# Attention and feed-forward on one core: softmax denominators of several tiles in one step, a joint transpose of the tails, another planned order

## The chip, the cores and the metric

The kernel runs on one core of one Trainium2 chip. The metric is the device time of one execution in microseconds (us), the median of three runs. Before the change it is 660.17 us (659.78 to 661.85).

## What is computed

First attention for 4 batches of 8 heads, 576 positions of 64 features, causal, mixed with a linear memory term by a gate of each head. Then a feed-forward network from 512 over 2048 back to 512 features, with a rational activation, on all 2304 tokens.

```python
def _attn_ref(q, k, v, M_prev, z_prev, beta):
    scores = scale * np.matmul(q, k.transpose(0, 1, 3, 2))
    scores = np.where(causal, -1000000000.0, scores)
    scores = scores - scores.max(-1, keepdims=True)
    a = np.exp(scores)
    a /= a.sum(-1, keepdims=True) + 1e-09
    local = np.matmul(a, v)
    q_p = phi(q)                       # x + 1 above zero, exp(x) below
    mem_out = einsum(q_p, M_prev) / (einsum(q_p, z_prev) + 1e-06)
    return g * mem_out + (1 - g) * local

def _moe_ref(x, w_in, w_out, a, b):
    h = x @ w_in
    P = a[0] + a[1] * h + a[2] * h * h + a[3] * h * h * h
    Q = 1.0 + np.abs(b[0]) * np.abs(h) + np.abs(b[1]) * h * h
    return (P / (Q + 1e-06)) @ w_out
```

The weights of the feed-forward network come as 64-bit floats.

## The kernel before

Attention works on 16 **units**, a unit being two heads of one batch. `load` fetches a unit. `prep` turns q and k with matmuls against the identity (tile `idf`) into `kt`, and makes the memory term's `f` out of `E` (exp), `nk` (reused for relu) and `den` (the normaliser). The 576 queries of a head are four tiles of 128, t = 0 to 3, and a tail of 64. `tiles01` does t = 0 and 1, `tile23` does 2 and 3 one by one, and `tail` does the 64 last queries of both heads together.

`prob` is the softmax of one tile of one head. A DVE instruction (`TENSOR_TENSOR_REDUCE`, shown as `ISA` or `CUSTOM_DVE_ANT_0`) masks and takes the extreme, and a second one reads the accumulator into the small tile `st`. ACT takes the exponential (`P` or the smaller `Ps`) with its sum. POOL or DVE adds 1e-9 and multiplies with the head's gate (L617, L618). DVE takes the reciprocal (L620). POOL, ACT or DVE multiplies the row with it (L621 to L623). PE turns the result (L476), a copy brings it to `g`, and `av` multiplies with v and the memory term and leaves the unit's outcome in `x`, which `spill` stores to DRAM (`xs`).

The feed-forward network works in two **halves** of eight of the 16 slices of 2048. For every slice `weights` makes two 32-bit parts of a weight (`ta`, `tw`, `xf`, a PSUM bank). `group` loads 256 tokens (`xload`), multiplies (`ffn1`), runs the activation (`act_chain`, 36 chains in the first half and 36 in the second), multiplies with the second weight (`ffn2`), and stores a partial sum `po`. The second half adds to it and writes the result. With `full` set, `act_chain` computes one factor with an ACT instruction (L828) and a POOL product (L492), else with one DVE instruction (L498). `FULL = 4` sets it for all groups from the fourth in the first half; the second half always has it.

The order is not written by hand. `Sched.place` is a planner. It knows a price for every operation (`c_act`, `c_dve`, `c_pool`, `c_mm4` ...) and a priority (`PRI`), puts the operation first that can start first, chooses among the engines that an operation may run on by its price times one plus `BIAS`, and so lays down one instruction queue for each engine. Each queue is then run in that order. SP issues all DMAs, in its own queue.

## Time and profile before

| | us |
|---|---|
| median of 3 runs | 660.17 |
| the profiled execution | 659.89 |
| its span, first to last instruction | 658.1 |

| engine | busy us | share of the span |
|---|---|---|
| PE (matmul) | 630.4 | 96% |
| DVE | 530.2 | 81% |
| ACT | 444.0 | 67% |
| POOL | 452.1 | 69% |

The span has three parts. Until about 160 us there is attention alone, with the splitting of the first half's weights beside it. Until about 290 us attention and the first matmuls of the feed-forward network are mixed. From then on there is the network alone, to 658 us. A busy PE is not a PE at its peak: matmuls overlap, and a slow stream of them can count as busy. How many start in a stretch says more.

### The profile page before, as it was taken

How to read it: one execution, taken by the hardware profiler on the slowest of the kernel's cores; microseconds unless marked ns; L12 is line 12 of the kernel's file. 1: busy time of each engine (PE TensorE's matmuls, PEld its weight loads, DVE VectorE, ACT ScalarE, POOL GpSimd, SP SyncE). 2: the span in 40 equal slices, each digit the busy share in tenths (PEclk: the TensorE clock that was granted, in tenths of full speed). 3: DMA queues.
4: the chain of work that ended last, by engine and by line, in shares of the span. 5: the costliest groups of instructions: out<-in, count | busy, mean ns of one | idle time of the engine just before them, and what ended most of it. 6: DMA issues, size and time to landing. Idle time of an engine off the chain costs nothing.

```text
span 658.1 us, 11480 instructions
## 1 busy us (share of the span) xinstructions
PE 630.4 (96%) x3744; PEld 496.7 (75%) x3744; DVE 530.2 (81%) x1229; ACT 444.0 (67%) x987; POOL 452.1 (69%) x553
## 2 busy tenths in 40 slices
PE   5999989789999999999999999999999999999997
PEld 3656555446776777788999999998998888888876
DVE  4899999986997775958999979789887767677765
ACT  3899799787789787664575766677465555372671
POOL 3778688886665755744677979888766666475563
PEclk9999999799999999999999999999999999999999
DMA  5644755557231421226464334222771110300301
GB/s 116 167 125 118 197 161 155 170 140 205 75 90 35 126 79 37 85 80 234 151 193 142 117 126 160 81 81 96 282 297 31 64 65 1 127 2 0 129 0 65
DMA packets 89276, 75.74 MB, mean 115 GB/s; under 512 B 62592, under 2 KB 75392, under 8 KB 86912
## 3 DMA queue, kind: packets, MB, share of 16 engines
q1 hardware_dynamic: 89216, 75.00, 36.9%
q8 instruction: 30, 0.49, 0.3%
q14 instruction: 30, 0.25, 0.1%
HBM read 51.39 MB, written 23.59 MB: 114 GB/s over the span
## 4 chain that ended last, share of the span: by engine, by line
PE 74%; DVE 9%; ACT 7%; POOL 5%; issue 2%; DMA 2%; SPq 1%; POOLq 0%; ACTq 0%; DVEq 0%
PE bk L465 68%; PE bk L476 6%; DVE bk L605 2%; ACT Ps L609 1%; ACT g L470 1%; ACT P L609 1%; POOL Ps L621 1%; DMA xf<-in_moe_w_in_dram 1%; SPq L458 1%; POOL nk L492 1%; DVE E L498 1%; POOL st L617 1%; DVE tb L819 1%; POOL E L492 1%; DVE bk L783 1%
## 5 line engine op out<-in xcount | busy, mean ns | idle before, releaser
L465 PE MATMUL bk<-xg,w 128*128 128x256 f32 x864 | 111.0, 285 | 0.0
L465 PEld LDWEIGHTS bk<-xg,w 128*128 128x128 f32 x864 | 106.8, 191 | 2.7 <-issue 1.5
L492 POOL TENSOR_TENSOR tw<-tw,gh 128x512 f32<-128x512 f32 x56 | 72.8, 1301 | 42.2 <-DVE gh L498 37.8
L814 POOL TENSOR_SCALAR tw<-ta,cb 128x512 f32<-128x512 f32 x68 | 53.7, 789 | 63.7 <-ACT ta L810 63.6
L492 POOL TENSOR_TENSOR tw<-tw,ta 128x512 f32<-128x512 f32 x72 | 94.0, 1306 | 4.3
L465 PE MATMUL bk<-w,gh 128*128 128x512 f32 x288 | 90.5, 395 | 0.0
L810 ACT ACTIVATE ta<-bk 128x512 f32<-128x512 f32 x72 | 43.0, 597 | 68.8 <-PE bk L465 32.8
L465 PE MATMUL bk<-w2o,gh 128*128 128x512 f32 x288 | 88.7, 390 | 0.0
L605 DVE CUSTOM_DVE_ANT_0 bk<-bk,mk 128x384 f32<-128x384 f32 (+3 forms) x144 | 71.5, 520 | 8.2 <-PE bk L465 8.0
L818 ACT ACTIVATE ta<-tw,lnb 128x512 f32<-128x512 f32 x72 | 52.0, 722 | 33.9 <-POOL tw L492 33.5
L819 DVE TENSOR_TENSOR tb<-bk,tb 128x512 f32<-128x512 f32 x72 | 49.3, 686 | 30.6 <-ACT tb L811 25.9
L498 DVE SCALAR_TENSOR_TENSOR bk<-bk,ca,tw 128x512 f32<-128x512 f32 x72 | 54.2, 753 | 18.7 <-POOL tw L492 18.4
L465 PE MATMUL bk<-w,w2i 128*128 128x512 f32 x288 | 67.7, 390 | 0.0
L470 ACT COPY g<-bk 128x384 f32<-128x384 f32 (+2 forms) x128 | 58.2, 496 | 7.4 <-PE bk L476 6.4
L821 DVE SCALAR_TENSOR_TENSOR bk<-tb,ca,bk 128x512 f32<-128x512 f32 x72 | 54.0, 750 | 11.3 <-ACT ta L810 10.5
L465 PEld LDWEIGHTS bk<-w,w2i 128*128 128x128 f32 x288 | 53.9, 188 | 11.7 <-DVE gl L834 0.5
L811 ACT ACTIVATE tb<-bk,ca 128x512 f32<-128x512 f32 x59 | 45.6, 773 | 24.1 <-PE bk L465 23.9
L465 PEld LDWEIGHTS bk<-w2o,gh 128*128 128x128 f32 x288 | 53.6, 188 | 10.7
L465 PEld LDWEIGHTS bk<-w,gh 128*128 128x128 f32 x288 | 52.2, 188 | 11.4 <-issue 1.1
L498 DVE SCALAR_TENSOR_TENSOR gh<-bk,ca,ta 128x512 fp32r<-128x512 f32 x72 | 53.5, 743 | 8.5 <-ACT ta L823 4.5
L465 PE MATMUL bk<-w2o,gl 128*128 128x512 f32 x144 | 56.1, 390 | 1.2 <-DVE gl L834 1.2
L465 PE MATMUL bk<-w,gl 128*128 128x512 f32 x144 | 56.1, 389 | 0.0
(123 smaller groups left out, 1413.4 us busy)
## 6 DMA issues: line engine op xcount, KB each, us to landing
xh<-xg SPq DMA_DIRECT2D x9, 1024.0 KB, 5.0
xf<-in_moe_w_in_dram SPq DMA_DIRECT2D x16, 512.0 KB, 4.3
xf<-in_moe_w_out_dram SPq DMA_DIRECT2D x16, 512.0 KB, 3.4
w<-xh SPq DMA_DIRECT2D x6, 1024.0 KB, 11.9
xs<-x SPq DMA_DIRECT2D x16, 288.0 KB, 2.2
xf<-xs SPq DMA_DIRECT2D x9, 512.0 KB, 6.1
po<-tb SPq DMA_DIRECT2D x18, 256.0 KB, 2.8
pi<-po SPq DMA_DIRECT2D x18, 256.0 KB, 2.8
```

The lines of the kernel that those rows point to most:

```text
L465: T.matmul(o, lhsT=l, rhs=r, start=s0, stop=s1, skip_group_check=more)
L470: sc.op([("act", c_act(n), lambda: A.copy(out=out(), in_=in_())), ("dve", c_dve(n), lambda: V.tensor_copy(out(), in_()))], reads, writes, pri)
L476: T.matmul(o, lhsT=i, rhs=idn, start=x == 0, stop=True, is_transpose=True, skip_group_check=x > 0)
L492: opts = {"pool": ("pool", c_pool2(n), lambda: G.tensor_tensor(**kw()), "t"), "dve": ("dve", c_dve(n), lambda: V.tensor_tensor(**kw()), "2")}
L498: return dve(c_dve(n) + 61 * ap, lambda: V.scalar_tensor_tensor(out=out(), in0=in0(), scalar=scalar() if callable(scalar) else scalar, in1 ...
L605: V.tensor_tensor_reduce(out=s, in0=s, in1=m, scale=-0.125, scalar=st.t[:, 0:1] if x else 3.0e38, op0=ALU.add, op1=ALU.min, accum_out=st.t ...
L810: act(c_act(N), lambda: A.activation(a_(), h(), AF.Abs), [(hb, None)], [(ta, None)], p)
L811: sc.op([("act", c_act(N, ap=2), lambda: A.activation(b_(), h(), AF.Identity, scale=ca[:, 3:4], bias=ca[:, 2:3])), ("dve", c_dve(N) + 61, ...
L814: sc.op([("pool", c_pool(N, 2), lambda: G.tensor_scalar(w_(), a_(), cb[:, 1:2], cb[:, 0:1], op0=ALU.mult, op1=ALU.add), "s"), ("act", c_ac ...
L818: act(c_act(N, False, 1), lambda: A.activation(a_(), w_(), AF.Ln, scale=2.0 ** -63, bias=lnb[:, 0:1]), [(tw, None)], [(ta, None)], p)
L819: dve(c_dve(N), lambda: V.tensor_tensor(out=b_(), in0=h(), in1=b_(), op=ALU.mult), [(hb, None)], [(tb, None)], p)
L821: dve(c_dve(N) + 61, lambda: V.scalar_tensor_tensor(out=h(), in0=b_(), scalar=ca[:, 1:2], in1=h(), op0=ALU.add, op1=ALU.mult), [(tb, None) ...
```

## The change

`prob` now takes a list of tiles. For t = 0 and 1 the four tiles of both heads share one `st`, and one DVE instruction (L630, `SCALAR_TENSOR_TENSOR`) adds 1e-9 to all four sums and multiplies with the gates, and one reciprocal (L632) serves all four. For t = 2 and 3 two tiles share them. This step is now on DVE alone. The tails of q and k are loaded into one tile `kq` (k in the upper half, q in the lower half) and turned with one matmul in the place of two. q's tail is loaded once more into `nq`, for the exponential. `x` becomes `x0` and `x1`, each stored as soon as it is there. One weight operation (an absolute value) may run on DVE too. `FULL` is 10, so that the first half's chains all take the DVE instruction. The planner's price of a pair of matmuls of two heads loses a surcharge of half (`1.5 * c_mm4(n)` becomes `c_mm4(n)`), and `BIAS` and `PRI` are new numbers, in a loop over half units.

```diff
-BIAS = {'act': 1.73, 'dve': 2.43, 'pool': -0.41}
+BIAS = {'act': 0.23, 'dve': 2.22, 'pool': -2.16}
...
+        for i, src in enumerate((k, q)):
+            dma(lambda i=i, src=src: (kq.t[64 * i:64 * i + 64].rearrange("p (a d) -> p a d", a=2), src[bb, h2, SM:S, :].rearrange("a p d -> p a d")),
+                [], [(kq, i)], pri, 64 * 512, 256)
...
-        tr(lambda: [(b4(tl)[:, x, :], ad(s, 4), idf) for x, s in enumerate((nk, nq))],
-           2 * 109, [(nq, None), (nk, None)], [(tl, None)], p, [kt, qd])
+        tr(lambda: [(tl.t[:, 0:128], kq.t, idf)], 109, [(kq, None)], [(tl, None)], p, [kt, qd])
...
-        sc.op([("pool", c_pool(1, 1), lambda: G.tensor_scalar(st.t[:, 4:5], st.t[:, l], 1e-9, gcol, op0=ALU.add, op1=ALU.mult), "s"),
-               ("dve", 130, lambda: V.tensor_scalar(st.t[:, 4:5], st.t[:, l], 1e-9, gcol, op0=ALU.add, op1=ALU.mult))],
-              [(st, ("l", mx))], [(st, "r")], p)
-        dve(75, lambda: V.reciprocal(st.t[:, 5:6], st.t[:, 4:5]), [(st, "r")], [(st, "i")], p)
...
+        def den():
+            x = col(1).rearrange("p (t i) -> p t i", i=gcol.shape[1])
+            y = col(2).rearrange("p (t i) -> p t i", i=gcol.shape[1])
+            V.scalar_tensor_tensor(out=y, in0=x, scalar=1e-9, in1=gcol.unsqueeze(1).to_broadcast(list(x.shape)), op0=ALU.add, op1=ALU.mult)
+        dve(130, den, [(st, ("l", 0, k)) for k in range(w)], [(st, "r")], p)
+        dve(75, lambda: V.reciprocal(col(3), col(2)), [(st, "r")], [(st, "i")], p)
...
-        mm(f, 1.5 * c_mm4(n) + 100, [(kt, "k"), (kt, "q")], [(x, None) for x in bk], p, take=P[0] + P[1])
...
+            mm(f, c_mm4(n) + 100, [(kt, "k"), (kt, "q")], [(x, None) for x in bk], p + t, take=P + [st])
...
-        x = d["x"] = d.get("x") or sc.buf("x")
-        copy(n, lambda: x.t[:, q0:q0 + n], lambda: o.t[:, 0:n], [(o, None)], [(x, ch)], p)
...
+        x = sc.buf(f"x{ch}")
+        copy(n, lambda: x.t, lambda: o.t[:, 0:n], [(o, None)], [(x, None)], p)
+        dma(lambda: (xs[c, :, bb * S + q0:bb * S + q0 + n], x.t), [(x, None)], [(ex(("xs", bb, ch)), c)], p, 128 * n * 4)
...
-FULL = 4
+FULL = 10
...
-PRI = {'load': 21.6, 'head': 19.6, 'av0': 13.5, 'prep': 46.6, 't2': 52.0, 'tail': 15, 'av1': 75.9, 'w': 50.2, 'w2': 3401.0, 'group': 218.5, 'chain': 10.9, 'ahead': 366.1, 'ahead2': 6071.5, 'last': 3553.7}
+PRI = {'load': 4.5, 'head': 2.3, 'av0': 13.2, 'prep': 25.3, 't2': 14.8, 't3': 2.5, 'tail': -9.4, 'av1': 42.9, 'w': 100.2, 'w2': 6715.7, 'group': 227.8, 'chain': 22.8, 'ahead': 329.1, 'ahead2': 2903.3, 'last': 1385.4}
```

Three places of the order show what moves. The first is DVE's queue in the softmax of a middle unit; `st` is the tile of sums, `g` the gates. Before:

```order
L618 TENSOR_SCALAR st_166<-st_166,g_92 128x1
L605 ISA bk_113,st_170<-bk_113,mk 128x512
L605 ISA st_170 128x1
L620 RECIPROCAL st_166<-st_166 128x1
L620 RECIPROCAL st_167<-st_167 128x1
L605 ISA bk_118,st_170<-bk_118,mt,st_170 128x64
L605 ISA st_170 128x1
L781 TENSOR_SCALAR bk_115<-ta_179 128x512
L620 RECIPROCAL st_168<-st_168 128x1
```

After:

```order
L807 TENSOR_SCALAR bk_115<-ta_179 128x512
L809 SCALAR_TENSOR_TENSOR bk_115<-xf_194,bk_115 128x512
L630 SCALAR_TENSOR_TENSOR st_162<-st_162,g_92 128x4
L614 ISA bk_116,st_166<-bk_116,mk 128x512
L614 ISA st_166 128x1
L632 RECIPROCAL st_162<-st_162 128x4
L614 ISA bk_113,st_166<-bk_113,mk 128x512
L614 ISA st_166 128x1
```

Four gate steps (this one on DVE, the others on POOL) and four reciprocals became one of each, four columns wide. In the whole program the reciprocals fall from 144 to 64, the gate steps from 144 (62 on DVE, 82 on POOL) to 64, all on DVE.

The second place is POOL's queue, where a unit's rows are multiplied with the reciprocal. Before:

```order
L621 TENSOR_SCALAR P_149<-P_149,st_162 128x512
L621 TENSOR_SCALAR P_150<-P_150,st_163 128x512
L617 TENSOR_SCALAR st_164<-st_164,g_92 128x1
L621 TENSOR_SCALAR Ps_153<-Ps_153,st_159 128x128
L617 TENSOR_SCALAR st_165<-st_165,g_92 128x1
L621 TENSOR_SCALAR Ps_155<-Ps_155,st_164 128x128
L621 TENSOR_SCALAR Ps_154<-Ps_154,st_165 128x256
L617 TENSOR_SCALAR st_166<-st_166,g_92 128x1
```

After:

```order
L506 TENSOR_SCALAR w_177<-tw_186 128x512
L494 TENSOR_TENSOR w_177<-tw_186,w_177 128x512
L636 TENSOR_SCALAR Ps_157<-Ps_157,st_163 128x128
L636 TENSOR_SCALAR Ps_158<-Ps_158,st_163 128x128
L636 TENSOR_SCALAR Ps_155<-Ps_155,st_163 128x256
L636 TENSOR_SCALAR P_153<-P_153,st_167 128x512
L636 TENSOR_SCALAR P_152<-P_152,st_167 128x512
```

The small gate steps are gone from POOL's queue, and the products of a group of tiles stand in a row.

The third place is PE's queue at the end of attention (`mz`, `nv`: the last products of the last unit; `xg,w`: first matmuls of the feed-forward network; `w,gh`: its second ones). Before:

```order
L465 MATMUL bk_113<-xg_195,w_177 128x256 x12
L465 MATMUL bk_114<-xg_195,w_177 128x256 x24
L476 MATMUL bk_115<-idf,P_152 128x128 x4
L476 MATMUL bk_116<-idf,P_150 128x128 x4
L465 MATMUL bk_112<-xg_195,w_177 128x256 x12
L465 MATMUL bk_111<-f_144,mz_138 128x320
L465 MATMUL bk_111<-g_174,vt_130 128x64
L465 MATMUL bk_111<-g_174,nv_128 64x320 x6
L465 MATMUL bk_111<-g_174,nv_128 64x192 x2
```

After:

```order
L467 MATMUL bk_113<-w_177,gh_187 128x512 x2
L467 MATMUL bk_113<-w_177,gl_190 128x512
L467 MATMUL bk_117<-f_146,mz_140 128x320
L467 MATMUL bk_117<-g_172,vt_132 128x64
L467 MATMUL bk_117<-g_172,nv_130 64x320 x6
L467 MATMUL bk_117<-g_172,nv_130 64x192 x2
L467 MATMUL bk_118<-xg_195,w_177 128x256 x24
L467 MATMUL bk_114<-xg_195,w_177 128x256 x24
L467 MATMUL bk_111<-xg_195,w_177 128x256 x24
```

Before its last attention matmul PE had 252 feed-forward matmuls of 256 columns and 48 of 512 columns in its queue; now it has 96 and 9. The others moved behind attention.

## Rows read from the trace of the kernel before

**Rows 1.** Stretches of the span, all engines; columns named in the first row.
```profile
core 0: us, PE busy (x) PEld busy (x) DVE busy (x) ACT busy (x) POOL busy (x), PEclk, DMA share, GB/s
...
20.00:80.00 60.00, 58.15 (x379) 36.69 (x379) 54.58 (x189) 52.13 (x156) 45.30 (x73) 1.00 0.57 148
80.00:140.00 60.00, 51.09 (x299) 30.58 (x299) 57.33 (x183) 51.74 (x151) 50.53 (x74) 0.94 0.60 169
140.00:160.00 20.00, 18.03 (x118) 11.17 (x117) 14.96 (x63) 15.72 (x53) 17.31 (x27) 1.00 0.59 164
160.00:290.00 130.00, 128.34 (x870) 93.75 (x871) 101.06 (x322) 101.10 (x271) 79.43 (x123) 1.00 0.28 80
290.00:480.00 190.00, 190.00 (x1216) 172.47 (x1215) 164.74 (x246) 119.99 (x191) 146.01 (x137) 1.00 0.44 152
480.00:614.00 134.00, 134.00 (x649) 113.17 (x648) 96.10 (x140) 70.22 (x108) 78.32 (x71) 1.00 0.21 75
```

**Rows 2.** The chain that ended last: start us, us, what.
```profile
207.52 2.80 PE bk L476 x24
...
289.59 325.15 PE bk L465 x1868
...
627.27 27.22 PE bk L465 x118
```

**Rows 3.** Waits of DVE, 80 to 140 us: us in total, times, longest.
```profile
DVE st L620 <- POOL st L617: 0.7, 3, 0.4
```

**Rows 4.** DVE groups by line and form: count, busy us, mean ns, idle before.
```profile
L620 DVE RECIPROCAL st<-st 128x1 f32<-128x1 f32 x144 | 20.9, 154 | 8.1 <-POOL st L617 7.2
...
L498 DVE SCALAR_TENSOR_TENSOR tw<-tw,gh 128x512 f32<-128x512 f32 x16 | 15.2, 949 | 0.3
...
L618 DVE TENSOR_SCALAR st<-st,g 128x1 f32<-128x1 f32 x58 | 11.3, 202 | 3.2 <-ACT Ps L609 2.7
...
L812 DVE TENSOR_SCALAR tb<-bk,ca 128x512 f32<-128x512 f32 x13 | 10.5, 807 | 8.1 <-ACT ta L810 7.7 <-PE bk L465 0.2
...
L575 DVE TENSOR_SCALAR nk<-nq 128x640 f32<-128x640 f32 x12 | 6.9, 577 | 0.4 <-PE bk L476 0.2
L623 DVE TENSOR_SCALAR Ps<-Ps,st 128x128 f32<-128x128 f32 x8 | 5.0, 626 | 0.0
L615 DVE TENSOR_TENSOR st<-st 128x1 f32<-128x1 f32 x16 | 4.9, 305 | 1.7 <-ACT P L609 1.7
L623 DVE TENSOR_SCALAR Ps<-Ps,st 128x256 f32<-128x256 f32 x6 | 4.8, 796 | 0.0
```

**Rows 5.** Line L615: instructions' duration in ns, min/median/max.
```profile
L615 DVE TENSOR_TENSOR st<-st x16: 135/156/1301, 16.6 to 247.3; 128x1 f32<-128x1 f32 x16
```

**Rows 6.** ACT and POOL groups, same columns as rows 4.
```profile
L811 ACT ACTIVATE tb<-bk,ca 128x512 f32<-128x512 f32 x59 | 45.6, 773 | 24.1 <-PE bk L465 23.9
L828 ACT ACTIVATE tw<-tw,lnb 128x512 f32<-128x512 f32 x56 | 39.7, 710 | 0.0
...
L574 ACT ACTIVATE nk<-nq 128x640 f32<-128x640 f32 x4 | 3.1, 766 | 0.0
...
L492 POOL TENSOR_TENSOR tw<-tw,gh 128x512 f32<-128x512 f32 x56 | 72.8, 1301 | 42.2 <-DVE gh L498 37.8 <-ACT ta L810 2.8 <-ACT ta L818 1.6
...
L617 POOL TENSOR_SCALAR st<-st,g 128x1 f32<-128x1 f32 x70 | 20.2, 288 | 28.0 <-ACT Ps L609 9.6 <-ACT P L609 9.1 <-DMA nv<-in_v_dram 4.5
```

**Rows 7.** SP's queue near the start: start us, us of issuing, what.
```profile
2.55 1.91 SPq L458 DMA_DIRECT2D nk<-in_k_dram  x3
```

**Rows 8.** PE's timeline at 401 us: 24 matmuls of 256 columns, until the next.
```profile
400.97 3.04 PE L465 MATMUL bk<-xg,w 128*128 128x256 f32 x24
403.84 0.63 PE L465 MATMUL bk<-w,gh 128*128 128x512 f32 x2
```

**Rows 9.** All engines, 520 to 540 us, 512-column matmuls alone; columns as rows 1.
```profile
520.00:540.00 20.00, 20.00 (x90) 16.57 (x89) 12.52 (x19) 10.43 (x16) 10.97 (x11) 1.00 0.12 40
```

More of the change, by code (lines that the diff above doesn't have):

```diff
@@ L563, in prep @@
             r = slice(64 * i, 64 * i + 64)
[L564 removed]
+            copy(64, lambda r=r: qd.t[r, r], lambda r=r: tl.t[r, 64:128], [(tl, None)], [(qd, i)], p)
         for src, n, c0 in ((nk, "k", 0), (nq, "q", S)):
@@ L640, in tiles01 @@
     def tiles01(u, p):
         d = ST[u]
-        P = [scores(u, t, p + t) for t in range(2)]
+        P = scores(u, (0, 1), p)
         g = d["g0"] = sc.buf("g0")
@@ L654, in tile23 @@
         n = 128 * (t + 1)
-        P = scores(u, t, p)
+        P = scores(u, (t,), p - t)
         if "g1" not in d:
@@ L704, in f @@
             return [(a_, l, r, x == 0, x == len(L) - 1) for x, (a_, l, r) in enumerate(L)]
-        mm(f, c_mm4(n) + sum(c_mm4(n - o0) for o0 in blk) + 0.5 * c_mm4(n) + (c_mm4(64) if ch else 0) + 100,
+        mm(f, c_mm4(n) + sum(c_mm4(n - o0) for o0 in blk) + (c_mm4(64) if ch else 0) + 100,
            [(g, None), (nv, None), (vt, None), (mz, None), (F, None)], [(o, None)], p, more=True)
-        x = d["x"] = d.get("x") or sc.buf("x")
-        copy(n, lambda: x.t[:, q0:q0 + n], lambda: o.t[:, 0:n], [(o, None)], [(x, ch)], p)
@@ L710, in spill @@
-    def spill(u, p):
-        bb, c = divmod(u, KC)
-        x = ST[u]["x"]
-        dma(lambda: (xs[c, :, bb * S:(bb + 1) * S], x.t), [(x, None)], [(ex(("xs", bb)), c)], p, 128 * S * 4)
-    pr = PRI
-    load(0, -1)
-    prep(0, 0)
-    for u in range(U):
-        base = 100.0 * u
-        if u + 1 < U:
-            load(u + 1, base + pr["load"])
-        tiles01(u, base + 10)
-        av(u, 0, base + pr["av0"])
-        if u + 1 < U:
-            prep(u + 1, base + pr["prep"])
-        for t in range(2, 4):
-            tile23(u, t, base + pr["t2"] + pr["head"] * (t - 2))
-        tail(u, base + pr["tail"])
-        av(u, 1, base + pr["av1"])
-        spill(u, base + pr["av1"] + 2)
+        x = sc.buf(f"x{ch}")
@@ new lines, in av @@
+        copy(n, lambda: x.t, lambda: o.t[:, 0:n], [(o, None)], [(x, None)], p)
+        dma(lambda: (xs[c, :, bb * S + q0:bb * S + q0 + n], x.t), [(x, None)], [(ex(("xs", bb, ch)), c)], p, 128 * n * 4)
+    pr = PRI
+    units = []
+    for bb in range(NB):
+        us = range(KC * bb, KC * bb + KC)
+        units += [(x, u) for x in "AB" for u in us] if bb < SWEEPS else [(x, u) for u in us for x in "AB"]
+    pos = [j for j, x in enumerate(units) if x[0] == "A"]
+    load(0, -100)
+    prep(0, -60)
@@ new lines, in tile_attention_ffn @@
+    for at, (kind, u) in enumerate(units):
+        base = 50.0 * at
+        for j in pos:
+            if j and at == j - (1 if j - 1 in pos else 2):
+                load(units[j][1], base + pr["load"])
+            if j and j - 1 == at and kind == "B":
+                prep(units[j][1], base + pr["prep"])
+        if kind == "A":
+            tiles01(u, base + pr["head"])
+            av(u, 0, base + pr["av0"])
+            if at + 1 in pos:
+                prep(units[at + 1][1], base + pr["prep"])
+        else:
+            for t in range(2, 4):
+                tile23(u, t, base + pr["t2"] + pr["t3"] * (t - 2))
+            tail(u, base + pr["tail"])
+            av(u, 1, base + pr["av1"])
@@ L839, in xload @@
         xf, xg = sc.buf(tf), sc.buf(tg)
-        rd = [(ex(("xs", bb)), None) for bb in range(t0 // S, (t0 + 255) // S + 1)]
+        rd = {(x // S, int(x % S >= 256)) for x in (t0, t0 + 255)}
+        rd |= {(b1, c1) for b1, _ in rd for c1 in range(2) if t0 < b1 * S + 256 * (1 + c1) + 64 * c1 and t0 + 256 > b1 * S + 256 * c1}
+        rd = [(ex(("xs", *x)), None) for x in sorted(rd)]
         dma(lambda: (xf.t, xs[:, :, t0:t0 + 256].rearrange("c p s -> p c s")), rd, [(xf, None)], p, 128 * KC * 1024)
```

109 lines of the change are left out of this document (61 added, 48 removed).

## The prediction

> **What bounds the kernel now.** I read the stretches first, for every engine side by side. From 290 to 614 us PE is busy all the time [rows 1], and the chain of waits there is one piece of 325 us of matmuls [rows 2]. So the last part is bound by PE, and nothing that another engine gains in it is worth anything. What can be won lies before 290 us.
>
> There PE's busy share misleads: 58.2 of 60 us, 51.1 of 60, 128.3 of 130 [rows 1]. Busy counts slow streams too, so I count matmul starts. Both stretches from 20 to 80 and from 80 to 140 us hold attention alone, in about the same mixture. The first starts 379 matmuls (6.3 in a us), the second 299 (5.0 in a us) [rows 1]. At the first pace 299 matmuls take 47.3 us, so 12.7 of the 60 us are lost against it; the 118 of 140 to 160 us lose another 1.3. Who is late? From 80 to 140 us DVE is busy 57.3 of 60 us, ACT 51.7, POOL 50.5 [rows 1], and DVE hardly waits: the longest row of its waits there is 0.7 us [rows 3]. DVE sets the pace of this middle, where the splitting of the weights stands beside the softmax. From 20 to 80 us it is closer: DVE 54.6, ACT 52.1 [rows 1], and neither has much to spare. From 160 to 290 us PE is busy all but 1.7 us, with feed-forward matmuls as filling.
>
> **The change part by part.** My base is the profiled execution, 659.9 us (a span of 658.1 and 1.8 around it); the median of the runs is 0.3 above it.
>
> *PE.* One transpose less in each of 16 units: 24 transposes in a row take 2.80 us [rows 2], 0.117 each, so 16 take 1.9 us. PE waits for none of it elsewhere, so I take it in full: **-1.9**. Everything else on PE is the same work in another order.
>
> *The moved feed-forward matmuls.* Before the last attention matmul PE had 252 of 256 columns and 48 of 512; now 96 and 9. 24 of the first kind take 2.87 us until the next instruction starts [rows 8], 0.120 each; 90 of the second take 20 us [rows 9], 0.222 each. 156 x 0.120 + 39 x 0.222 = 27.4 us that leave the stretch before 290 us and come back behind it, where PE never waits. The sum is nothing, as long as attention ends 27.4 us (with the transposes 29) earlier than at 289.6 us [rows 2]: the point on which all turns. If the engines beside PE cannot follow, what is missing is lost one for one.
>
> *DVE in attention.* Off: 80 reciprocals of 0.154 (12.3 us), 62 gate steps of 0.202 (12.5), 12 relus of 0.577 that go to ACT (6.9) [rows 4], and, by the order, 17 of 23 row products that go to POOL or ACT, 0.63 to 0.80 each for the most part [rows 4], some 12. Together 44 us. On: 64 gate steps with two tensors from SBUF, which the trace does not show in that form. The nearest row is L615, also two small inputs from SBUF on DVE: 0.156 in the median, 0.305 in the mean, 1.301 at worst [rows 4, 5]. By the median 10 us, by the mean 19.5; I take the mean, since POOL's products stand beside them as they stand beside L615. Net -24 to -34, I take -25, which is 1.6 us for a unit. What stands behind such a step on DVE is the next mask and the next exponential.
>
> The tail of L615 is a wait, not work: 1.301 is POOL's product of 1301 ns [rows 6] once over. The Trainium skill, page "SBUF — State Buffer", section "Who interferes with whom", says that a DVE instruction with two SBUF inputs contends with a GpSimd instruction that reads SBUF. Its rule speaks against moving 82 gate steps off POOL onto DVE in this form, where the old form (one tensor, 0.202) has a steady price; the trace agrees with it as far as L615 shows. If every step waited out a POOL product, 64 x 1.3 = 83 us would land on DVE, by rows; the mean of L615 makes that unlikely, and it only enters the upper end.
>
> *ACT in attention.* On: 12 relus of 0.766 [rows 6] and some copies and row products, 12 us in all by the order's counts, 0.75 for a unit. *POOL*: off 82 gate steps of 0.288 (23.6 us) [rows 6], on some 15 row products, so it has room.
>
> *What that is worth.* From 80 to 140 us there are 3.3 units, so DVE falls from 57.3 by 5.3 to 52.0; ACT rises from 51.7 by 2.5 to 54.2 and is next late. If ACT can be packed as DVE was (57.3 of 60), the 60 us become 56.7; over the 88 us from 72 to 160 a gain of 4.9. The order also spreads the weights' DVE work over more units (up to the twelfth, where it was done by the tenth), which takes ACT and DVE load out of the middle: up to the whole 14 us that the pace of 20 to 80 us would give. Between 0 and 14 I take **-6**, near the row of ACT, because it is the one that I can count. In the first 72 us, four units, ACT and DVE were about even, and ACT's 0.75 a unit at 87% busy (52.1 of 60) costs 0.86 each: **+3.5**, from 0 to 3.5.
>
> *Start.* Two small loads of `kq` now stand ahead of k. Before, a small and two large ones took 1.91 us of issuing [rows 7], 0.64 each, so k comes 0.6 us later. The tails' scores go ahead meanwhile. I take it in the 3.5.
>
> *SP.* 32 more DMAs (16 halves of `x`, 16 tails of q) at 0.64 are 20 us of issuing in 260, in a queue that mostly waits. `xs` waits for a copy of `x`, and behind it stand the loads of units to come; with two stores it can wait twice, the first one earlier. I cost it at nothing; the bound is +3 where a load comes late.
>
> *The first half's chains.* 20 more `tw` steps on DVE of 0.949, and 13 steps of 0.807 that go to ACT: +8.5 us on DVE from 290 to 480 us, where it is busy 164.7 of 190. ACT gives up 20 of 0.710 and takes 13 of 0.773 [rows 4, 6], POOL gives up 20 of 1.301. DVE comes to 91%, PE stays fed from chains ahead, so nothing; if that cover is gone, up to +8.
>
> Sum: 659.9 - 1.9 - 6 + 3.5 = 655.5, and 0.3 for the median: **about 655 us**.
>
> **The rivals.** *A, ACT becomes the bound, slower.* ACT has to do 0.75 us more for each unit, and feed-forward filling, which hid such waits from 160 to 290 us, is cut from 300 matmuls to 105. If ACT, at 87% busy, sets the pace of all 16 units, attention ends 16 x 0.86 = 13.8 us late and DVE's relief buys nothing: 659.9 - 1.9 + 13.8 + 0.3 = 672. It decides as soon as attention ends later than 289.6 - 27.4 = 262 us. For it: ACT comes to 54.2 of 60 us in the middle, more than any other engine. Against it: DVE is still the one that hardly waited. With half of it the time is 665.
>
> *B, nothing changes.* The lost pace of the middle is PE's own small matmuls and not a wait, or the freed time is eaten by the chain from sums to reciprocal to product, which now waits for the last of four exponentials. The granted clock is part of it: 0.94 in that stretch and 1.00 beside it [rows 1], after PE had waits that left it idle for 8.9 of the 60 us; 6% of 60 us are 3.6 of the 12.7. Then only the transposes count: 658.3. Against it: the starts fall from 6.3 to 5.0 in a us exactly where DVE is fullest.
>
> *C, the whole loss of the middle comes back.* The planner's lower price for pairs lets PE and the other engines fit more closely, ACT costs nothing, and the 14 us return: 659.9 - 1.9 - 14 + 0.3 = 644.
>
> **How the numbers follow.** Chances: the forecast 0.38, A 0.29, C 0.18, B 0.15. The range goes from C with some more, 642, to A's 670. About 0.3% (2 us) is what a measurement of this kernel can tell from no change, so faster is under 658.2. The forecast brings 0.33 of its 0.38 there, C all, B 0.06: 0.57. Within 0.3%: 0.15, most of it B and the forecast's edge. Slower: 0.28, all A.
>
> **What would show it.** The forecast is right if the last attention matmul ends near 258 us, if from 80 to 140 us PE starts some 320 attention matmuls or more, and if DVE is no longer over 55 of 60 us there. The 16 transposes show in the count of `kq`. If the new gate steps take over 0.4 us in the mean, the DVE term is wrong. If ACT is over 56 of 60 us from 20 to 140 us and attention ends after 262 us, A is right. If PE waits for DVE's `gl` between 290 and 480 us, the first half's chains have lost their cover. The prediction is wrong at its root if PE is not busy all the time after attention.

## The result, and the profile after

The changed kernel takes **642.29 us** (median; 642.08 to 642.89), the kernel before 660.38 beside it: a ratio of 0.9724, 95% interval 0.9707 to 0.9742. The change is 18 us faster, not 5. The time lies inside the range, 12.7 us from the forecast, and close to rival C's 644. The profiled execution took 642.24 us, 17.7 less than the one of before (659.9).

Stretches of the changed kernel, all engines, as [rows 1]:

```profile
core 0: us, PE busy (x) PEld busy (x) DVE busy (x) ACT busy (x) POOL busy (x), PEclk, DMA share, GB/s
20.00:80.00 60.00, 56.34 (x362) 34.91 (x360) 49.82 (x162) 55.98 (x160) 39.80 (x56) 1.00 0.58 148
80.00:140.00 60.00, 57.81 (x388) 37.71 (x387) 56.04 (x177) 56.77 (x173) 47.89 (x63) 1.00 0.64 163
140.00:160.00 20.00, 17.85 (x112) 10.82 (x110) 19.00 (x62) 17.58 (x52) 14.90 (x21) 1.00 0.67 172
160.00:250.00 90.00, 89.90 (x627) 62.31 (x627) 63.31 (x220) 79.13 (x230) 62.36 (x83) 1.00 0.34 94
250.00:290.00 40.00, 40.00 (x267) 37.04 (x268) 32.16 (x50) 23.14 (x36) 22.38 (x22) 1.00 0.53 172
290.00:480.00 190.00, 190.00 (x1211) 173.26 (x1210) 171.38 (x252) 109.27 (x173) 129.38 (x124) 1.00 0.44 153
```

The middle is another one: from 80 to 140 us PE starts 388 matmuls where it was 299, at a granted clock of 1.00 where it was 0.94. DVE still stands at 56.0 of 60 us and ACT has come up beside it, 56.8 where it was 51.7. The 0.94 is one stretch of the kernel before at the lower of the clock's two levels (1.2 and 2.4 GHz); the changed kernel has none. Columns as above:

```profile
100.00:117.50 17.50, 15.92 (x95) 9.36 (x95) 16.17 (x46) 16.16 (x46) 13.42 (x23) 1.00 0.58 158
...
117.50:124.30 6.80, 4.41 (x15) 2.64 (x14) 6.40 (x20) 5.07 (x13) 6.53 (x8) 0.50 0.75 219
```

PE had stood idle for 1.6 of the 17.5 us before the clock fell. Half of the 6.8 us, 3.4, is the most that the clock took there. Behind 250 us PE is busy without a gap, as it was behind 290.

The chain of waits of the changed kernel (start us, us, what), its last long piece, as [rows 2]:

```profile
245.03 391.35 PE bk L467 x2228
```

It begins 44.6 us earlier than the piece of before (289.59). The feed-forward matmuls that moved behind attention take 27.4 us. The difference, 17.2, is nearly the whole gain of 17.7. So the question is why attention ran faster, and where. The table follows attention alone, counted from the matmul starts in both traces: the time at which the n-th eighth of all attention matmuls had been started, less the feed-forward matmuls started by then (0.120 and 0.222 us each, the prediction's prices). Eighths are of each kernel's own count (1440 attention matmuls, or 1424 with one transpose of the tails). The last four columns are runs that are told of below.

```
eighth   before   after | h_w50   n_w75   g_w100   w_soft
1         40.9     39.3 |  38.2    39.8    42.8     40.2
2         68.8     70.5 |  69.4    71.0    70.3     73.9
3        100.8     99.6 | 101.1   101.0   101.4    106.8
4        139.0    128.8 | 139.8   129.9   131.6    141.5
5        168.7    157.0 | 166.9   162.3   160.4    175.3
6        197.1    184.0 | 196.2   190.5   192.9    206.7
7        223.5    209.9 | 224.5   216.7   219.3    233.4
8        252.6    236.1 | 253.3   244.2   247.0    261.7
```

The first half is 10.2 us shorter, nearly all of it in the fourth eighth (38.2 us before, 29.2 after). The second half is 6.3 shorter (113.6 and 107.3). Together 16.5 of the 17.7 us.

What left the middle can be read from DVE's four steps on the weights there, 80 to 140 us (rows as [rows 4]), before and after:

```profile
L779 DVE TENSOR_SCALAR ta<-ta 128x512 f32<-128x512 f32 x10 | 9.2, 922 | 0.5 <-ACT ta L777 0.4
...
L783 DVE SCALAR_TENSOR_TENSOR bk<-xf,bk 128x512 int32<-128x512 int32 x11 | 7.7, 704 | 0.0
L781 DVE TENSOR_SCALAR bk<-ta 128x512 int32<-128x512 int32 x11 | 7.6, 690 | 0.4 <-ACT f L470 0.4
L786 DVE SCALAR_TENSOR_TENSOR tw<-xf,bk 128x512 int32<-128x512 int32 x10 | 6.8, 680 | 0.0
```
```profile
L809 DVE SCALAR_TENSOR_TENSOR bk<-xf,bk 128x512 int32<-128x512 int32 x8 | 5.7, 709 | 0.1
L812 DVE SCALAR_TENSOR_TENSOR tw<-xf,bk 128x512 int32<-128x512 int32 x8 | 5.5, 684 | 0.0
...
L807 DVE TENSOR_SCALAR bk<-ta 128x512 int32<-128x512 int32 x7 | 4.9, 698 | 0.1
L805 DVE TENSOR_SCALAR ta<-ta 128x512 f32<-128x512 f32 x7 | 4.2, 603 | 0.1
```

They take 31.3 us before and 20.3 after. What is left of DVE's busy time rises from 26.0 to 35.7 us, by 37%, and PE's starts by 30%: DVE's attention work for each matmul did not fall, the weights made room for more of it.

### The profile page after: what moved, and what is told of

It reads as the page before. It is cut to its first block, busy times and chain, and to the rows that moved or that the text cites. A ratio compares the mean times of both kernels' runs of the same rounds, so it can differ in the third digit from the quotient of the medians.

```text
span 640.0 us, 11414 instructions
## 1 busy us (share of the span) xinstructions
PE 620.2 (97%) x3728; PEld 494.0 (77%) x3728; DVE 509.5 (80%) x1121; ACT 442.7 (69%) x993; POOL 419.3 (66%) x475
## 4 chain that ended last, share of the span: by engine, by line
PE 87%; ACT 5%; DVE 3%; DMA 2%; issue 1%; SPq 0%; POOL 0%; ACTq 0%; POOLq 0%; DVEq 0%
PE bk L467 79%; PE bk L478 9%; DMA xf<-in_moe_w_in_dram 2%; ACT g L472 1%; ACT kt L472 1%; DVE bk L614 1%; ACT Ps L620 1%; DVE st L630 1%; ACT P L620 1%; ACT nk L579 1%; DMA kq<-in_q_dram 0%; DMA kq<-in_k_dram 0%; DVE bk L809 0%; ACT ta L802 0%; DVE tw L812 0%
## 5 line engine op out<-in xcount | busy, mean ns | idle before, releaser
L840 POOL TENSOR_SCALAR tw<-ta,cb 128x512 f32<-128x512 f32 x71 | 57.1, 804 | 91.6 <-ACT ta L836 91.5
L467 PE MATMUL bk<-xg,w 128*128 128x256 f32 x864 | 108.5, 284 | 0.0
L494 POOL TENSOR_TENSOR tw<-tw,ta 128x512 f32<-128x512 f32 x72 | 95.9, 1332 | 4.5
L467 PE MATMUL bk<-w,gh 128*128 128x512 f32 x288 | 89.2, 391 | 0.0
L614 DVE CUSTOM_DVE_ANT_0 bk<-bk,mk 128x256 f32<-128x256 f32 (+3 forms) x144 | 71.6, 523 | 19.5 <-PE bk L467 17.4
L837 ACT ACTIVATE tb<-bk,ca 128x512 f32<-128x512 f32 x72 | 55.7, 774 | 22.9 <-PE bk L467 22.8
L494 POOL TENSOR_TENSOR tw<-tw,gh 128x512 f32<-128x512 f32 x36 | 46.6, 1295 | 35.6 <-DVE gh L500 34.0
```

Source lines behind the costliest of these rows:

```text
L467: T.matmul(o, lhsT=l, rhs=r, start=s0, stop=s1, skip_group_check=more)
L494: opts = {"pool": ("pool", c_pool2(n), lambda: G.tensor_tensor(**kw()), "t"), "dve": ("dve", c_dve(n), lambda: V.tensor_tensor(**kw()), "2")}
L614: V.tensor_tensor_reduce(out=s, in0=s, in1=m, scale=-0.125, scalar=st.t[:, k:k + 1] if x else 3.0e38, op0=ALU.add, op1=ALU.min, accum_out= ...
L837: sc.op([("act", c_act(N, ap=2), lambda: A.activation(b_(), h(), AF.Identity, scale=ca[:, 3:4], bias=ca[:, 2:3])), ("dve", c_dve(N) + 61, ...
L840: sc.op([("pool", c_pool(N, 2), lambda: G.tensor_scalar(w_(), a_(), cb[:, 1:2], cb[:, 0:1], op0=ALU.mult, op1=ALU.add), "s"), ("act", c_ac ...
```

## The experiments

All ratios are to the kernel before on the same chip; what one kernel costs or gains against another is the difference of their ratios times 660 us. *Order kept* means that every queue holds the changed kernel's order and only what an instruction does, or which engine does it, is edited. *Planned again* means that the planner made a new order from edited numbers; the operations stay, but some may land on another engine.

**Is it the lighter softmax work, or the order?** Two runs edit the changed kernel with its order kept, two plan it again with one old number.

`f1_single`: the gate step and the reciprocal of each tile by itself on DVE.
```diff
-V.scalar_tensor_tensor(out=y, in0=x, scalar=1e-9, in1=gcol..., op0=ALU.add, op1=ALU.mult)
+for k in range(w):
+    V.tensor_scalar(st.t[:, 2*w+k:...], st.t[:, w+k:...], 1e-9, gcol[:, j:j+1], op0=ALU.add, op1=ALU.mult)
-V.reciprocal(col(3), col(2))
+for k in range(w):
+    V.reciprocal(st.t[:, 3*w+k:...], st.t[:, 2*w+k:...])
```


> The changed kernel, its order kept on every engine, but the gate step and the reciprocal of a group of softmax tiles are issued tile by tile on DVE again (144 of each in the place of 64). That is 80 more reciprocals of 0.154 us and 80 more steps of 0.202 us on DVE in attention, up to 28 us in all, 1.8 us a unit. Theory W (what won is the lighter DVE queue in the middle of attention): 8 to 15 us slower than the changed kernel, 650 to 657. Theory O (what won is the planned order, with its prices and its postponed feed-forward matmuls): at most 3 us slower, 642 to 645.

Measured 642.32 us, 0.9708 [0.9691, 0.9724]: no cost at all, as theory O has it. That grouping saves steps is worth nothing in this order.

`f2_relu_dve`: all 16 relus on DVE (12 were there before the change, none after it).
```diff
-A.activation(R.t, nq.t, AF.Relu)
+V.tensor_scalar(R.t, nq.t, 0.0, None, op0=ALU.max)
```


> The changed kernel, its order kept, but all 16 relus on DVE (0.577 us) and not on ACT (0.766 us). From 20 to 140 us ACT is busy 112.8 of 120 us in the changed kernel and DVE 105.9. If ACT is now the bound of attention: 2 to 5 us faster, 637 to 640. If DVE still is (theory W in its plain form): 3 to 6 us slower.

Measured 645.96, 0.9762 [0.9736, 0.9788], 2.5 us more, with intervals that just touch. In the trace attention ends 3.7 us later (the last long piece of the chain starts at 248.73). Its stretch, columns as above:

```profile
80.00:140.00 60.00, 56.44 (x355) 34.86 (x353) 58.37 (x174) 51.62 (x161) 45.49 (x61) 0.97 0.57 147
```

With ACT at 51.6 of 60 us and DVE at 58.4 PE falls to 355 starts. So ACT's load, taken off and put on DVE, costs rather than gains, a little less than the 3 to 6 us of theory W. Whether ACT by itself bounds this order is not shown, since DVE got the load.

`f5_price` and `f6_bias`: the changed kernel planned again with the old price of a paired matmul, and with the old BIAS.
```diff
-mm(f, c_mm4(n) + 100, ...)
+mm(f, 1.5 * c_mm4(n) + 100, ...)
```
```diff
-BIAS = {'act': 0.23, 'dve': 2.22, 'pool': -2.16}
+BIAS = {'act': 1.73, 'dve': 2.43, 'pool': -0.41}
```


> The changed kernel, planned again with the old price for pairs of matmuls (1.5 times, and the half on top in the second product); the work is the same, the order another: 192 and 42 feed-forward matmuls of 256 and 512 columns stand before the last attention matmul, in the place of 96 and 9. Theory O: 6 to 15 us slower, 648 to 657. Theory W: within 3 us, 640 to 645.

> The changed kernel, planned again with the old weights for the choice of engine (ACT 1.73, DVE 2.43, POOL -0.41), which sends some relus and row products back to DVE. Theory O: 4 to 10 us slower, since the order with these weights is another. Theory W: 2 to 6 us slower by the work that goes back to DVE, and in the trace DVE over 57 of 60 us in the middle.

Measured 657.67, 0.9938 [0.9924, 0.9953], and 651.9, 0.9852 [0.9835, 0.9869]. The same operations in another order, in `f6_bias` partly on other engines, lose 14 and 8 of the 18 us. So the order carries much of the gain; but is it these numbers, or does any new plan lose?

**Does any new plan lose?** `n1_prio` moves two due times by one (`load` 4.5 to 5.5, `prep` 25.3 to 24.3); `n2_price11` raises the price of pairs by a tenth.
```diff
-PRI = {'load': 4.5, 'head': 2.3, 'av0': 13.2, 'prep': 25.3, ...}
+PRI = {'load': 5.5, 'head': 2.3, 'av0': 13.2, 'prep': 24.3, ...}
```
```diff
-mm(f, c_mm4(n) + 100, ...)
+mm(f, 1.1 * c_mm4(n) + 100, ...)
```


> Control for re-planning: the changed kernel with its new prices, but two due times of the planner moved a little (load 4.5 to 5.5, prep 25.3 to 24.3) and the order planned again from them; work, buffers and prices are as in the changed kernel, 96 and 9 feed-forward matmuls stand ahead of the last attention matmul. Theory O (the right price of a paired matmul is what makes the order good): the time stays within 4 us of the changed kernel, 641 to 646. Theory L (the order is good only at the numbers that were tuned for it, and any other set loses what the runs with the old price and the old bias lost): 648 to 657.

> The changed kernel planned again with the price of a paired matmul raised by a tenth, where the run with the old price had it half as high again (657.7). Theory O with the price as cause, in proportion: a fifth of 15 us, 644 to 647. Theory L (any new plan loses): 648 to 657. If the price itself matters little and both losses were the luck of a plan, it can come out anywhere from 640 to 657, with no order between this run, the one with the old price and the one with moved due times.

`n1_prio` took 640.84, 0.9694 [0.966, 0.9729], not to be told from the changed kernel; `n2_price11` 652.64, 0.9866 [0.9841, 0.9891], which lies in theory L's range. A new plan need not lose, so theory L falls as it was put, for any plan. But a tenth more on the price costs 9 us where half as much again costs 14: the price does not act in proportion, so the loss is not that of a wrong estimate alone, and a small change of a number can cost 9 us.

**Does the price alone do it?** `g1_price`: the kernel before with the new price and nothing else.
```diff
-mm(f, 1.5 * c_mm4(n) + 100, ...)
+mm(f, c_mm4(n) + 100, ...)
```


> The kernel before with one thing of the change alone: the planner's price of paired matmuls goes from 1.5 times to once the single price; softmax per tile, two transposes of the tails, one x, the old due times and bias stay, and the order is planned again (216 and 51 feed-forward matmuls ahead of the last attention matmul). Theory O with the price as cause: most of the 18 us without any change of work, 643 to 650. Theory O with price and due times only together: 652 to 658. Theory L (numbers tuned for the old price fit no other): 658 to 668.

Measured 665.81, 1.0065 [1.0045, 1.0084]: slower than before, in theory L's range. The price is not the cause by itself.

**The old work in the new order.** `w_all` joins the edits of `f1_single`, `f3_full` and `f4_two_tr`.


> The new order with the old work: the changed kernel's order and queues kept instruction for instruction, but the factor of the softmax is again made for each tile by itself, on POOL the gate step and on DVE the reciprocal, k's and q's tails are again turned by two transposes, and the steps of the splitting that the change moved to DVE and POOL by its higher FULL go back to ACT and POOL from the fourth group on. Theory O (the order is the gain): 2 us for the transposes and little else, 643 to 647. Theory W (the lighter softmax is the gain, in sum if not by the DVE steps alone): 650 to 660, as most of the 18 us goes with the work.

One thing in this text is not what ran: the kernel had the single gate step on DVE, not on POOL. Measured 656.6, 0.9926 [0.9899, 0.9953], 13 us above the changed kernel and in theory W's range; theory O does not allow it. The two runs that take it apart, order kept:

`f3_full`: the chains' third step from the fourth group on.
```diff
-stt(N, w_, w_, 1.0 + 1e-6, lambda: rb(h_()), ALU.add, ALU.mult, ...)
+A.activation(w_(), w_(), AF.Identity, bias=lnb[:, 2:3])
+G.tensor_tensor(out=w_(), in0=w_(), in1=rb(h_()), op=ALU.mult)
```
`f4_two_tr`: the transpose of `kq` twice.
```diff
-[(tl.t[:, 0:128], kq.t, idf)]
+[(tl.t[:, 0:128], kq.t, idf), (tl.t[:, 128:256], kq.t, idf)]
```


> The changed kernel with its order kept, and one thing of the old work alone: from the fourth group on the third step of a splitting chain runs on ACT and POOL again (FULL as before), not on DVE. In the run with all old work, PE was short of work by 8 us between 290 and 480 us, where POOL stood at 142 of 190 us. Theory F (the moved steps are what keeps PE fed behind attention, now that fewer chains are ready when attention ends): the larger part of that run's 14 us comes with this edit, 650 to 656. Rival (the steps cost nothing, as PE never waited there in the kernel before; the 14 us come from the softmax steps on POOL and the transposes): 642 to 645.

> The changed kernel with its order kept and the transpose of kq issued twice in each of the 16 units, the second into a part of the bank that nobody reads. By the prediction's term PE pays 16 x 0.117 = 1.9 us in full: 644 to 645. If PE has slack ahead of 245 us, which the matmul starts of the middle suggest, nothing: 641.5 to 643.

`f3_full` took 655.56, 0.9919 [0.9901, 0.9938]; `f4_two_tr` 643.12, 0.9739 [0.9718, 0.976]. So the chain steps alone lose as much as `w_all`, and none of that lies in attention: in `f3_full` the last eighth ends at 236.0 us, as in the changed kernel (236.1). PE starves behind it. Its stretch, and what PE waited for there (us in total, times, longest):

```profile
290.00:480.00 190.00, 182.71 (x1118) 164.34 (x1117) 146.91 (x218) 111.20 (x178) 141.69 (x135) 0.97 0.42 145
```
```profile
PE bk L467 <- POOL xg L494: 4.0, 4, 1.5
PE bk L467 <- ACT tb L958: 3.1, 2, 2.9
```

PE is idle for 7.3 of the 190 us, and that is not all: twice in this stretch the granted clock stands at its lower level, once right behind a wait of 1.5 us and once from within one of 2.9.

```profile
415.40:418.80 3.40, 3.40 (x19) 3.40 (x18) 1.45 (x2) 1.90 (x4) 1.95 (x3) 0.50 0.64 263
439.30:446.10 6.80, 5.94 (x19) 5.07 (x20) 3.95 (x6) 3.35 (x6) 3.79 (x3) 0.50 0.22 80
```

Matmuls of 256 columns start 0.21 us apart there, and 0.12 beside it; by these starts the clock adds some 4 us (an estimate).

Is this the price of the steps, or of an order that was laid out without them? `k_full4` plans again.
```diff
-FULL = 10
+FULL = 4
```


> The changed kernel with FULL back at 4 and the order planned again, where the run with the old chain steps had kept an order planned without them. The attention part of the plan stays as it is (96 and 9 feed-forward matmuls ahead of its last matmul, the weights' steps spread alike). If the 13 us of that run were the steps themselves (ACT and POOL do in two what DVE does in one, and POOL's copies of xg stand behind them): 651 to 657. If they were an order that did not suit the steps: 642 to 647.

Measured 641.6, 0.9698 [0.967, 0.9727], a little below the 642 to 647 expected of the second case. Planned for, the old chain steps cost nothing. The 13 us were a mismatch of order and work, and the same caution holds for the next run.

`w_soft`: `f1_single` with the gate step on POOL, and `f4_two_tr`, order kept.
```diff
-    V.tensor_scalar(st.t[:, 2*w+k:...], st.t[:, w+k:...], 1e-9, gcol[:, j:j+1], op0=ALU.add, op1=ALU.mult)
+    G.tensor_scalar(st.t[:, 2*w+k:...], st.t[:, w+k:...], 1e-9, gcol[:, j:j+1], op0=ALU.add, op1=ALU.mult)
```


> The changed kernel with its order kept and all of the old softmax and transposing work put back, but not the chain steps: a gate step on POOL and a reciprocal on DVE for each tile by itself (144 of each), and two transposes a unit. Theory O (the order is the gain, the lighter work is not): 642 to 645. Theory W (the lighter work is most of the gain): 650 to 658, as in the run with all old work, whose loss would then not have come from the chain steps alone.

Measured 667.3, 1.0094 [1.0063, 1.0124], 24 us above the changed kernel, beyond even theory W's range. DVE's longest wait in sum up to 270 us (us in total, times, longest):

```profile
DVE st L637 <- POOL st L632: 32.8, 95, 1.7
```

The reciprocal stands right behind its gate step in DVE's queue, so DVE waits out POOL, and everything behind it on DVE waits too; attention ends 25.7 us later (the chain's last piece starts at 270.73). In this order the number of steps is free; a step between two DVE steps that another engine does is not. An order planned for it is the kernel before: with 82 gate steps on POOL, DVE waited for them 7.2 us in all [rows 4], 0.7 of it in the middle [rows 3]. What it would cost in the changed kernel planned for it stays open.

**What is it in the order?** One number of the planner bears on the middle directly: the eight pieces of weights that are split beside attention were due every 50.2, now every 100.2. `h_w50` sets it back in the changed kernel, `n_w75` half way, `g_w100` sets it forward in the kernel before; all planned again.
```diff
-PRI = {..., 'w': 100.2, ...}
+PRI = {..., 'w': 50.2, ...}
```


> The changed kernel with one constant changed and the order planned again: the eight pieces of the weights that are split beside attention are due every 50.2 (as before, half a unit apart), not every 100.2, so that up to 14 of their 64 DVE steps fall into one unit, where it was 9. Theory S (spreading the weights' DVE work over seven units, not four, gives back the middle): the stall of the middle returns, attention at its old pace, some 10 us of the 18 gone, 648 to 656, and DVE over 56 of 60 us from 80 to 140 us with under 350 matmul starts on PE. Rival (the weights' due time is of no matter, the rest of the order is): 640 to 645.

> The mirror of the last: the kernel before with this one constant changed, the weights due every 100.2 and not every 50.2, and the order planned again with the old price and the old work; the steps of the weights then spread over ten units with at most 8 in one (16 before). Theory S: the stall from 80 to 140 us goes, PE starts 340 matmuls or more there (299 before), the attention ends 30 us earlier with 19 us of feed-forward matmuls moved behind it: 646 to 654. Rival (the spread alone gives nothing, as ACT or the old price sets the pace): 657 to 664.

> The changed kernel with the weights due every 75.2, half way between 50.2 (658.7 us) and 100.2 (642.3 us), planned again; their steps on DVE spread over eight units with at most 9 in one, as many as in the changed kernel's fullest unit. If the fullest unit decides: 642 to 646. If the length of the spread decides, in proportion: 648 to 653. If the two runs at either end differ by luck of the plan and not by the spread: anywhere from 642 to 660, out of that row.

`h_w50`: 658.68, 0.9979 [0.9955, 1.0002]. `n_w75`: 648.98, 0.9809 [0.9779, 0.9838]. With the changed kernel's 642.29 the three stand in a row: the closer together the weights are due, the slower. `n_w75` lies where the length of the spread decides, not the fullest unit; `h_w50` is slower than either theory had it. `g_w100`: 653.43, 0.9896 [0.9874, 0.9918], 7 us gained from this one constant, as theory S has it. Three plans can fall into a row by chance, where a tenth on a price moves 9 us; so the traces have to show whether the weights' place is where the time goes.

Two of the four steps of a weight piece on DVE write or read the tile `ta`; their busy time shows how the pieces lie. DVE's instructions on `ta` alone, in the kernel before, in the changed one, and in `h_w50` (busy us and count; then clock, DMA share, GB/s):

```profile
100.00:120.00 20.00, 6.58 (x8) 0.94 0.61 166
120.00:140.00 20.00, 6.27 (x8) 0.89 0.59 171
```
```profile
100.00:120.00 20.00, 2.75 (x6) 1.00 0.60 154
120.00:140.00 20.00, 3.43 (x5) 1.00 0.56 141
140.00:160.00 20.00, 3.91 (x6) 1.00 0.67 172
```
```profile
100.00:120.00 20.00, 5.53 (x8) 0.91 0.63 170
120.00:140.00 20.00, 4.33 (x7) 1.00 0.61 163
```

And all engines, first `h_w50`, then `g_w100`:

```profile
80.00:140.00 60.00, 52.20 (x320) 31.72 (x317) 51.58 (x145) 51.36 (x151) 42.56 (x54) 0.97 0.62 167
```
```profile
80.00:140.00 60.00, 56.63 (x348) 34.33 (x348) 56.23 (x199) 52.32 (x163) 49.70 (x77) 1.00 0.49 128
160.00:200.00 40.00, 36.30 (x240) 23.54 (x239) 32.74 (x122) 32.49 (x98) 33.20 (x51) 0.96 0.56 159
```

Before, the weights sat thick between 100 and 140 us, and PE was slowest there. Put back in the changed kernel, the thick stretch comes back and with it the slow fourth eighth (38.7 us in the table, 29.2 in the changed kernel). Thinned in the kernel before, PE goes from 299 to 348 starts and the first half is 7.4 us shorter (131.6 for 139.0). One sign of theory S failed: DVE is at 51.6 in `h_w50`, not over 56. DVE is full only from 100 to 120 us there (18.74 of 20); that what the bunch delays stalls the others, and these DVE, is my reading and was not followed. In `n_w75` the slow eighth is the fifth, from 129.9 to 162.3 us (32.4 us, 28.2 in the changed kernel); its weights are thickest from 120 to 140 us (5.22 us on `ta`), which overlaps it in part. And `g_w100` gives back 1.8 us after its middle: PE has 36.3 of 40 us from 160 to 200, where the kernel before, with feed-forward matmuls as filling, has 39.8.

The weights' place does not cover the second half, though. `h_w50` loses 11.0 us in the first half of attention and 6.2 in the second, where its weights are all but done (0.69 us on `ta` from 140 to 160 us); `n_w75` loses 1.1 and 7.0. One thing moves with the times. By the matmul starts, 105 feed-forward matmuls stand ahead of the last attention matmul in the changed kernel, `n1_prio` and `k_full4` (642.3, 640.8, 641.6 us); 147 to 159 in `n2_price11`, `n_w75`, `h_due` and `f6_bias` (649 to 653); 234 in `f5_price` (657.7) and 369 in `h_w50` (658.7). All nine plans fall into these groups in the order of their times. Their activation chains need ACT, DVE and POOL beside the attention, which can slow it; but a slow attention also leaves room for more of them. No run separates the two, and the plans of the kernel before do not follow it (`g_w100_group`, below, has 108 and is slow).

**The other 11 us.** On `g_w100` two parts of the change were put, planned again: the grouped softmax, and the new price.


> The kernel before with the weights due every 100.2 and the softmax sums handled together (64 gate steps and reciprocals, all on DVE, as in the changed kernel), planned again with the old price, bias and due times. The spread alone gave 653.4. If the lighter softmax is worth something once the weights no longer fill DVE: 644 to 650. If it is worth nothing, as the run of the changed kernel with a gate step and a reciprocal for each tile says: 651 to 656.

> The kernel before with the weights due every 100.2 and the new price of paired matmuls, planned again; softmax, tails and x as before. The spread alone gave 653.4, the price alone 665.8. If the price pays once the weights are spread: 643 to 649. If it pays only with the new due times around it, as the price alone says: 651 to 660.

`g_w100_group` (the changed kernel's `prob` and `scores` in place of the old ones) took 661.71, 1.0014 [0.9988, 1.004], `g_w100_price` (the edit of `g1_price`) 669.84, 1.0125 [1.0095, 1.0155]. Both are worse than the spread alone (653.4), and slower than any of the ranges expected. Why the first is, was not followed; its attention ends 6.3 us later (253.3 us in the table's count, 247.0). The second loses most of it behind attention, where PE waits for DVE's `gl`; its stretch and that wait:

```profile
290.00:480.00 190.00, 180.52 (x1121) 161.94 (x1119) 157.14 (x233) 114.76 (x181) 141.34 (x133) 0.97 0.33 112
```
```profile
PE bk L465 <- DVE gl L834: 9.4, 3, 5.8
```

`h_due`: the changed kernel with other due times for attention, planned again. Seven of the eight are the old ones on the new base.
```diff
-'load': 4.5, 'head': 2.3, 'av0': 13.2, 'prep': 25.3, 't2': 14.8, 't3': 2.5, 'tail': -9.4, 'av1': 42.9,
+'load': 21.6, 'head': 10, 'av0': 13.5, 'prep': 46.6, 't2': 2.0, 't3': 19.6, 'tail': -35, 'av1': 25.9,
```


> The changed kernel with the attention's eight due times set back to what they were before, counted on the new base (a head pair's tail due 40 and its late rows 17 earlier in its unit than in the changed kernel, its preparation 21 later), and the order planned again; price, bias and the weights' due times stay as changed. If the attention's due times carry a good part of the gain that the spread of the weights does not explain: 650 to 660. If the spread of the weights is the whole: 641 to 646.

The edit does not do all that this text says. The preparation counts from the middle of a unit in the changed kernel, so its old time would be -3.4; at 46.6 it is due 21.3 later than in the changed kernel, where the kernel before had it 28.7 earlier. And the tail is due 25.6 earlier, not 40. Measured 650.72, 0.9833 [0.9796, 0.987], 7 us slower. That attention's due times matter is shown; what the old ones would cost is not.

## Why the prediction fell short

*Where the time is decided: right.* Nearly all of it, 16.5 of 17.7 us, is decided in attention. The moved feed-forward matmuls cost nothing, since PE's last long piece began at 245 us where 262 was enough, and PE is busy all the time behind it. The first half's chains cost nothing either: DVE came to 171.4 of 190 us, the 91% of the working came to 90. What the added DMAs of SP cost, put at nothing, no run tested. (The sum itself gives 655.8, not 655.)

*The transposes, -1.9: at most that.* Doubling them costs 1.0 us by the ratios, and the intervals of `f4_two_tr` and the changed kernel overlap, so it may be nothing.

*DVE in attention, -25 us of work: its price about right, its worth wrong.* The gate steps took less than the 0.4 us that I had set as the limit, but more than my 0.305. DVE's groups of the gate step (L630) and the reciprocal (L632) in the changed kernel, as [rows 4]:

```profile
L630 DVE SCALAR_TENSOR_TENSOR st<-st,g 128x2 f32<-128x2 f32 x32 | 12.6, 394 | 5.6 <-ACT P L620 3.5 <-ACT Ps L620 1.7
L630 DVE SCALAR_TENSOR_TENSOR st<-st,g 128x4 f32<-128x4 f32 x16 | 6.1, 380 | 1.4 <-ACT Ps L620 1.2
L630 DVE SCALAR_TENSOR_TENSOR st<-st,gtail 128x1 f32<-128x1 f32 x16 | 5.4, 340 | 0.1
...
L632 DVE RECIPROCAL st<-st 128x2 f32<-128x2 f32 x32 | 5.1, 158 | 0.4
...
L632 DVE RECIPROCAL st<-st 128x4 f32<-128x4 f32 x16 | 2.7, 167 | 0.0
L632 DVE RECIPROCAL st<-st 128x1 f32<-128x1 f32 x16 | 2.5, 156 | 0.1
```

The 64 grouped gate steps are 24.1 us, 0.377 each, where 58 single ones on DVE took 11.3 before and the rest stood on POOL [rows 4, 6]. With the reciprocals (10.3) that is 34.4 us, a little more than the 32.2 of [rows 4]. So grouping did not lighten DVE, and `f1_single`, with 23.7 us for 144 single gate steps, shows that it need not. The move from POOL, which I had put down as a cost for DVE and as room for POOL, ended a wait; in the kernel before that wait was 7.2 us in all [rows 4], and only in an order not made for it is it worth 24 (`w_soft`).

*The start, +3.5: about right, and taken back.* The first two eighths are 1.7 us longer, and the attention matmuls that the kernel before started by 72 us take 3.4 us longer; by the third eighth it is 1.2 shorter.

*The middle, -6: this is the step that failed.* The attention matmuls that the kernel before started from 72 to 160 us, in 88 us, take 72.4 in the changed kernel: 15.6 us, more than twice the term and beyond its bound of 14. What stands behind them is 4.3 shorter still, for which the sum had no term but the transposes. I had seen both causes, the lighter softmax and the spread of the weights, and the full 14 us as the bound of the second. I then took a value near ACT's row because ACT was what I could count: I let the engine that is next late set the pace, at 54.2 of 57.3, and put the spread of the weights at next to nothing. The rows of the changed kernel show DVE at 56.0 and ACT at 56.8 in the same 60 us, so one could be packed without hindering the other. And my sign for DVE (under 55 of 60) failed while the time was won: DVE stayed as full, but spent 11 us less of the stretch on weights and 10 more on attention.

*Rival A.* ACT did become the fullest engine, 55.98 and 56.77 of 60 us, as it said, and attention ended 17 us ahead of its point. When `f2_relu_dve` takes the load off ACT again, and puts it on DVE, the time gets no better. A fuller engine here went with a better-fed one.

*Rival B* fell with the 18 us. Its part on the clock came true the other way: the stretch at the lower level went with the waits, and with it at most 3.4 us, near the 3.6 it had.

*Rival C* had the time (644), not the cause. It named the price of pairs, which alone makes the kernel before slower (`g1_price`), on top of the spread too (`g_w100_price`).

**What is shown and what stays open.** Shown: most of the gain is the order's, since numbers of the planner alone take 7 to 17 us of it away, while the single softmax steps, the second transposes and (planned again) the old chain steps put back cost 0, 1 and 0; the weights' due time is part of it, 7 us in the kernel before, and in the changed kernel the slow fourth eighth returns where it is undone. That the spread acts by degree rests on three plans. Not shown: why the second half of attention got faster, and a sum. The weights' due time, the price, the BIAS and, moved as in `h_due`, attention's due times cost 17, 14, 8 and 7 us when each alone is changed, 46 in all for a gain of 18. It looks as if they were fitted to one another, and each pulls the plan out of it. Why the price has to be the new one for these due times, and the old one for the old, I can't say; and how far the gate step's move from POOL made such an order possible was not settled, as no run planned the changed kernel again with that step on POOL.

## What to carry to other kernels

Where a planner sets the order, work put beside a tight stage should come due at the pace at which that stage can carry it: one due time was worth 7 us by itself in the old kernel and 17 in the new. Ask of an edit not only how many us of work it takes off an engine, but whether a queue must wait for another engine in its middle. Do not judge a step by an edit that keeps an order made without it: such an edit cost 13 us that went away when it was planned for. After a change of order, compare the pace of the bound work itself (starts in each stretch, less what was moved), not busy shares: ACT was fuller after and DVE nearly as full, and the kernel faster.
